# Weights of the last experts on the software queue, a GpSimd drain in another place, and an earlier token table

## Chip, cores, metric

One core of one Trainium2 chip. The metric is device microseconds (us) of one execution. Each execution is called fast, or slow when it took over 1.5% longer than the fastest of the same kernel in the same series.

## The reference

Causal attention over 4 batches of 8 heads (768 positions, head size 64); three heads attend to the whole past, five to 4 first positions and a window of 64. The result is the token matrix of a mixture of experts: each token goes to the one expert its domain id names.

```python
x = attn_out.transpose(0, 2, 1, 3).reshape(B * S, H * D)     # 3072 x 512
for e in range(8):
    mask = domain_id == e
    h = np.maximum(x[mask] @ w1[e], 0.0)                     # 512 -> 1024
    out[mask] = h @ w2[e]                                    # 1024 -> 512
```

## The kernel before

Attention runs over 16 pairs of heads (TensorE scores, ScalarE exponentials, TensorE again). VectorE works out a token table beside it (ranks of tokens in their experts). Then GpSimd gathers each expert's rows with indirect DMAs, TensorE does two layers, VectorE copies each group of 128 output rows from PSUM (the memory space in which the program places TensorE's results) into one of six buffers, which is called evacuation below (0.69 us each in the profile of before), and GpSimd scatters the group to its places with an indirect DMA. `nc.gpsimd.drain()` is an instruction whose record lasted 22.46 us in the profile of before, and GpSimd stood idle from 168.6 to 190.5 us. "Layer 1" and "layer 2" below are the two matrix products of an expert. Weights are 32-bit in memory and 16-bit where TensorE reads them. Either they are converted on the way by GpSimd's software queue (14 DMAs of 1024 KB each on the page of before), or, for w2 of experts 6 and 7, they come as they are through SyncE's hardware queue into spare buffers ("staged", eight DMAs of 512 KB) and VectorE casts them (eight casts of 0.69 us).

```python
opool = ctx.enter_context(tc.tile_pool(name="moe_out", bufs=6))
ps_b = ctx.enter_context(tc.tile_pool(name="ps_b", bufs=2, space=PSUM))
# ... (cut)
def w2_stage(e):
    for x in range(4):
        # ... (a spare tile of the attention half, as 32-bit)
        nc.sync.dma_start(out=stage_t[e, x], in_=src[:, x // 2, x % 2 * F : (x % 2 + 1) * F])

def w2_cast(e):
    # ...
    for x in range(4):
        nc.vector.tensor_copy(out=flat[:, x * F : (x + 1) * F], in_=stage_t[e, x])

def finish_group(pr, g, ps, o=None):
    o = opool.tile([P, DM], FP32, tag="oute", name=f"oute_{pr}_{g}")
    nc.vector.tensor_copy(out=o[:], in_=ps[:])               # the evacuation of PSUM
    inst = nc.gpsimd.indirect_dma_start(out=out, ..., in_=o[:])   # the scatter
# ...
after = {                                                    # (expert, group of layer 2) just done
    (0, 2): lambda: load_w(3, 2),
    (1, 2): lambda: ([load_xe(3, g) for g in range(4)], load_w(6, 1),
                     [load_xe(3, g) for g in range(4, NG)], load_w(7, 1)),
    (2, 0): lambda: w2_stage(6),
    (2, 2): lambda: (load_w(4, 2), load_w(5, 2)),
    (3, 2): lambda: (nc.gpsimd.drain(), w2_cast(6), w2_stage(7)),
    (5, 1): lambda: w2_cast(7),
}
```

`load_w(e, 2)` issues w2 of expert e on the software queue. A key such as (3, 2) is written below for a drain's place too: after expert 3's third group (groups are counted from 0); "h" is the group of leftover rows that two experts share. The layers of experts 0 to 3 alternate with layer 1 of 4 to 7; after layer 1 of expert 7 only layer 2 of experts 4 to 7 is left, and that is the stretch this study is about.

The softmax here doesn't subtract the row's maximum and nothing guards it: scores larger than these inputs give would overflow.

Of the kernel before, what the change touches and what calls it, by code (L numbers as in the profile page):

```python
# [9 lines left out]
FP16 = mybir.dt.float16  # L10
FP32 = mybir.dt.float32
# [6 lines left out]
P = 128  # L18
# [3 lines left out]
def kernel(  # L22
# [13 lines left out]
    nc = tc.nc  # L36
    B, H, S, D = q.shape
    NTOK, DM = out.shape
    E, _, F = moe_w1.shape
# [66 lines left out]
    c32_d = nc.inline_tensor(c32_np, "c32").ap()  # L106
# [3 lines left out]
    wpool = ctx.enter_context(tc.tile_pool(name="weights", bufs=4))  # L110
    qkpool = ctx.enter_context(tc.tile_pool(name="qk", bufs=3))
    vpool = ctx.enter_context(tc.tile_pool(name="v32", bufs=4))
    vepool = ctx.enter_context(tc.tile_pool(name="ve", bufs=2))
    tpool = ctx.enter_context(tc.tile_pool(name="qkT", bufs=2))
    epool = ctx.enter_context(tc.tile_pool(name="eT", bufs=5))
    xpool = ctx.enter_context(tc.tile_pool(name="xb", bufs=2))
# [3 lines left out]
    ps_s = ctx.enter_context(tc.tile_pool(name="ps_s", bufs=3, space=PSUM))  # L120
    ps_b = ctx.enter_context(tc.tile_pool(name="ps_b", bufs=2, space=PSUM))

    c16 = cpool.tile([P, c16_np.shape[1]], FP16, name="c16s")
    c32 = cpool.tile([P, c32_np.shape[1]], FP32, name="c32s")
    dom64 = cpool.tile([P, NT], I64, name="dom64")
# [9 lines left out]
    q32_t, qk_t, v_t, ve_t, w_t = {}, {}, {}, {}, {}  # L135
# [4 lines left out]
    def load_qk(n):  # L140
        b, pi = divmod(n, 4)
        hA, hB = PAIRS[pi]
        for nm, src in (("q", q), ("k", k)):
            t = qkpool.tile([P, 2, NSO, D], FP32, tag=nm, name=f"{nm}32_{n}")
            nc.sync.dma_start(
                out=t[:].rearrange("p h t d -> p h (t d)"),
                in_=hsel(src, b, hA, hB).rearrange("h (p t) d -> p h (t d)", p=P),
            )
            q32_t[nm, n] = t
# [10 lines left out]
    def load_v(b, pi):  # L160
        hA, hB = PAIRS[pi]
        t = vpool.tile([P, 2, NSO, D], FP32, tag="v32", name=f"v32_{b}_{pi}")
        for hh, h in enumerate((hA, hB)):
            nc.sync.dma_start(
                out=t[:, hh], in_=v[b, h].rearrange("(c p) d -> p c d", p=P)
            )
        v_t[b, pi] = t
# [15 lines left out]
    def load_vs(r, bh):  # L183
# [3 lines left out]
                0:NS, 2 * H * (bh + 1) - VH : 2 * H * (bh + 1), :  # L187
            ],
        )

    stage_t = {}

    def w2_stage(e):
        for x in range(4):
            pool, tag = ((xpool, "xb"), (vepool, "ve"))[x % 2]
            t = pool.tile([P, 2 * F], FP16, tag=tag, name=f"w2s_{e}_{x}")
            stage_t[e, x] = t[:].bitcast(FP32)
            nc.vector.memset(stage_t[e, x][0:1, 0:1], 0.0)
            src = moe_w2[e].rearrange("(c p r) d -> p c (r d)", p=P, r=4)
            nc.sync.dma_start(out=stage_t[e, x], in_=src[:, x // 2, x % 2 * F : (x % 2 + 1) * F])  # L200

    def w2_cast(e):
        t = wpool.tile([P, 2, 4, DM], FP16, tag="w1", name=f"w2_{e}")
        flat = t[:].rearrange("p c r d -> p (c r d)")
        for x in range(4):
            nc.vector.tensor_copy(out=flat[:, x * F : (x + 1) * F], in_=stage_t[e, x])  # L206
        w_t[e, 2] = t

    def load_w(e, which):
        if which == 1:  # L210
            t = wpool.tile([P, 2, 2, F], FP16, tag="w1", name=f"w1_{e}")
            nc.gpsimd.dma_start(
                out=t[:].rearrange("p c r f -> p c (r f)"),
                in_=moe_w1[e].rearrange("(c p r) f -> p c (r f)", p=P, r=2),
            )
        else:
            tag = "w2" if e < 6 else "w1"
            t = wpool.tile([P, 2, 4, DM], FP16, tag=tag, name=f"w2_{e}")
            nc.gpsimd.dma_start(
                out=t[:].rearrange("p c r d -> p c (r d)"),  # L220
                in_=moe_w2[e].rearrange("(c p r) d -> p c (r d)", p=P, r=4),
            )
        w_t[e, which] = t
# [75 lines left out]
    qT, kT, eT, avp, xb = {}, {}, {}, {}, {}  # L299
# [133 lines left out]
    def routing_items():  # L433
        V = nc.vector
        R = {}
# [192 lines left out]
        def rows3():  # L628
# [19 lines left out]

        lows = [lambda t=t: low(t) for t in range(0, NT, 4)]
        return {  # L650
            (0, 1): (one_hot,), (0, 2): (ranks, scan), (1, 0): (own,), (1, 1): (place,),
            (2, 0): (place2,), (3, 0): (split,), (4, 0): (flags, high), (4, 1): (high2, high3),
            (4, 2): lows[0:1], (5, 1): lows[1:2], (8, 0): lows[2:3], (8, 1): lows[3:4],
            (8, 2): lows[4:5], (9, 1): lows[5:6], (10, 0): (rows,), (11, 0): (rows2,),
            (12, 0): (rows3,),
        }

    xe_t, xT_t, hT_t = {}, {}, {}
# [139 lines left out]
    nc.scalar.dma_start(out=c16[:, 0:C_S0], in_=c16_d[:, 0:C_S0])  # L798
    load_qk(0)
    load_v(0, 0)  # L800
    load_qk(1)
    nc.sync.dma_start(out=c16[:, C_S0:], in_=c16_d[:, C_S0:])
    nc.sync.dma_start(out=dom64[:], in_=moe_domain_id.rearrange("(p c) -> p c", p=P))
    nc.sync.dma_start(out=c32[:], in_=c32_d)
    load_v(0, 1)
    load_qk(2)
    load_v(0, 2)
# [39 lines left out]
                load_xe(1, g, 3)  # L847

    def keep_warm(m, tag):
        ps = ps_s.tile([P, 1024], FP32, tag="sp", name=f"warm_{tag}")  # L850
        for _ in range(m):
            nc.tensor.matmul(
                out=ps[:, 0:DM], lhsT=zrow[:, 0:P], rhs=zrow[:], start=True, stop=True
            )
# [8 lines left out]
    for n in range(NPAIR + 1):  # L863
        if n < NPAIR:
            hooks(n)
        R = len(plans[n % 4]) // 2 if n < NPAIR else 1
        av0, av1 = av_items(n - 1) if n >= 1 else ([], [])
        tr = []
        if n == NPAIR:
            av0 = [lambda: keep_warm(4, "exp")] + av0  # L870
            av1 = av1 + [lambda: keep_warm(6, "last"), lambda: x_transpose(0, 0, 1, wide=True)]
        elif n + 1 < NPAIR:
            q_evac = nc.scalar.copy if R == 1 else nc.vector.tensor_copy
            tr = [lambda: transposes(n + 1, q_evac, R == 1)]
        if R == 1:
            run(tr)
        steps = {1: [av0 + av1], 2: [tr, av0 + av1], 3: [tr, av0, av1] if n else [[], [], tr]}[R]
        for x, step in enumerate(steps):
            if n < NPAIR:
                scores(n, (2 * x, 2 * x + 1))  # L880
            run(step)
            for fn in route.get((n, x), ()):
                fn()
# [25 lines left out]
    for g in range(4, NG):  # L909
# [16 lines left out]
            [load_xe(3, g) for g in range(4, NG)],  # L926
            load_w(7, 1),
        ),
        (2, 0): lambda: w2_stage(6),
        (2, 2): lambda: (load_w(4, 2), load_w(5, 2)),  # L930
        (3, 2): lambda: (nc.gpsimd.drain(), w2_cast(6), w2_stage(7)),
        (5, 1): lambda: w2_cast(7),
    }
    then = lambda *k: after.get(k, lambda: None)()
    for pr in range(E // 2):
# [20 lines left out]
    with tc.If(nc.values_load(flag_i[0:1, 0:1], min_val=0, max_val=2) > 0, preferred_fallthrough_block=False):  # L956
        x_v = x_d[1 : 1 + NTOK, :].rearrange("(b p s) d -> b s p d", b=B, p=P)
        with tc.For_i(0, B, 1) as gb, tc.For_i(0, NSO, 1) as gs:
            t = gb * NSO + gs
            g_d64 = rpool.tile([P, 1], I64, name="g_d64")  # L960
            nc.sync.dma_start(
                out=g_d64[:], in_=moe_domain_id[bass.ds(t * P, P)].rearrange("(p c) -> p c", c=1)
# [6 lines left out]
            for c in range(4):  # L969
                c1, r = divmod(c, 2)  # L970
                nc.tensor.transpose(
                    out=gps[:, c, :],
                    in_=gx[:, c1 * 256 + r : (c1 + 1) * 256 : 2],
# [5 lines left out]
            for e in range(E):  # L979
# [14 lines left out]
                ps = ps_b.tile([P, 512], FP32, tag="b", name=f"go2_{e}")  # L994
                for f in range(8):
                    nc.tensor.matmul(
                        out=ps[:],
# [7 lines left out]
                    out=hit[:], in0=g_dom[:], scalar1=float(e), scalar2=None, op0=ALU.is_equal  # L1005
# [46 lines left out]
```

## Time and profile before

| | kernel before |
|---|---|
| timed | 223.49 us, median of 3 executions (222.88 to 225.37) |
| its first profile, one execution | 214.84 us, span 213.0 us |
| first matmul of layer 1 | 91.9 us |
| last activation of layer 1 (hT of expert 7) | 176.0 us |
| GpSimd drain | 167.19 to 189.65 us |
| TensorE's last matmul ends | 206.1 us |
| last scatter issued | 207.61 us |

### The profile page before, as it was taken

The numbers are of one execution on the slowest core, as the hardware profiler recorded it, in microseconds if no ns is written. First come the engines' busy times: TensorE is split into PE (matmuls) and PEld (weight loads), VectorE is DVE, ScalarE is ACT, GpSimd is POOL, SyncE is SP. The second block draws the span as 40 slices with busy tenths as digits, with TensorE's granted clock in tenths as the row PEclk, the third lists the DMA queues.
The fourth block names the chain that finished last, engine by engine and source line by source line (L and its number), as shares of the span: only waits on it lengthen the run. The fifth ranks groups of instructions, "written<-read, shape, count | busy, mean of one in ns | idle before, by whom it ended". The sixth has DMA issues, their size and how long they took to land.

```text
span 213.0 us, 5417 instructions
## 1 busy us (share of the span) xinstructions
PE 186.8 (88%) x2250; PEld 123.5 (58%) x2250; DVE 100.7 (47%) x216; ACT 90.4 (42%) x115; POOL 117.4 (55%) x152
## 2 busy tenths in 40 slices
PE   7589986699999899985999999999999999894950
PEld 2247664387678567685898965455555664342430
DVE  4357989956897886520012225310353412263320
ACT  2466577247986986333465620056200561000000
POOL 7726759683346468771788445557763400027771
PEclk9757999669999999999799999999999999999996
DMA  6999999999999997999999999997999999804532
GB/s 185 299 277 276 300 246 271 285 331 268 281 305 294 346 325 143 222 173 297 242 200 196 262 245 215 279 257 194 210 190 325 332 228 309 339 12 149 194 142 98
DMA packets 45056, 51.86 MB, mean 244 GB/s; under 512 B 28895, under 2 KB 37472, under 8 KB 45026
## 3 DMA queue, kind: packets, MB, share of 16 engines
q0 software_dynamic: 8928, 24.70, 50.2%
q1 hardware_dynamic: 35954, 26.70, 43.2%
q8 instruction: 19, 0.31, 0.6%
q10 hardware_dynamic: 144, 0.07, 0.3%
q14 instruction: 11, 0.09, 0.2%
HBM read 56.73 MB, written 10.49 MB: 316 GB/s over the span
## 4 chain that ended last, share of the span: by engine, by line
DMA 38%; PE 23%; issue 17%; DVE 11%; POOL 4%; ACT 3%; POOLq 1%; SPq 0%; DVEq 0%; ACTq 0%
DMA w<-in_moe_w_dram 25%; PE av L402 6%; DMA k<-in_k_dram 5%; PE sp L348 5%; DMA out_dram<-oute,out_i 5%; PE o L772 3%; DMA xe<-x_tok,map_e 3%; PE sp L331 3%; ACT eT L359 3%; PE tp L312 2%; DVE xb L415 2%; POOL out_dram L738 2%; DVE kT L321 2%; DVE qT L321 1%; POOL xe L672 1%
## 5 line engine op out<-in xcount | busy, mean ns | idle before, releaser
L359 ACT ACTIVATE eT<-sp 128x1024 f16<-128x1024 f32 (+2 forms) x56 | 50.1, 953 | 17.5 <-PE sp L348 17.2
L729 ACT ACTIVATE hT<-h 128x512 f16<-128x512 f32 (+2 forms) x48 | 32.1, 668 | 57.9 <-PE h L722 57.9
L722 PE MATMUL h<-xT,w 128*128 128x256 f16 (+2 forms) x384 | 52.1, 297 | 1.3 <-DVE xT L707 0.8
L738 POOL DMA_INDIRECT out_dram<-oute,out_i x27 | 27.5, 1017 | 42.9 <-DVE w L206 21.9
L722 PEld LDWEIGHTS <-w 128*128 128x128 f16 x384 | 39.6, 115 | 12.4 <-issue 0.9
L772 PE MATMUL o<-w,hT 128*128 128x512 f16 x184 | 42.0, 379 | 3.2 <-DVE oute L736 3.2
L736 DVE COPY oute<-o 128x512 f32<-128x512 f32 x23 | 15.9, 691 | 46.9 <-PE o L772 32.9
L772 PEld LDWEIGHTS <-hT 128*128 128x128 f16 x184 | 17.5, 98 | 23.1 <-issue 4.3
L402 PEld LDWEIGHTS <-eT 128*128 128x128 f16 (+2 forms) x672 | 21.4, 102 | 7.4 <-issue 4.9
L402 PE MATMUL av<-ve,eT 128*128 128x65 f16 (+2 forms) x572 | 22.9, 198 | 2.4 <-DVE qT L321 0.7
L155 POOL CAST q<-q 128x768 f16<-128x768 f32 x15 | 13.5, 901 | 19.4 <-DMA q<-in_q_dram 9.1
L348 PE MATMUL sp<-qT,kT 64*64 64x128 f16 (+8 forms) x468 | 22.1, 259 | 0.8 <-DVE kT L321 0.8
L672 POOL DMA_INDIRECT xe<-x_tok,map_i x16 | 16.3, 1016 | 10.2 <-DMA x_tok<-xb 5.6
L707 DVE COPY xT<-xtp 128x1024 f16<-128x1024 f16 (+1 forms) x16 | 8.8, 552 | 24.6 <-PE xtp L694 24.6
L415 DVE TENSOR_TENSOR xb<-av,rcp 128x384 f16<-128x384 f32 x32 | 17.8, 557 | 1.1
L155 POOL CAST k<-k 128x768 f16<-128x768 f32 x15 | 12.6, 839 | 9.9 <-PE sp L348 5.7
L331 PE MATMUL sp<-c16s 128*128 128x128 f16 (+2 forms) x112 | 17.2, 271 | 0.8 <-ACT eT L359 0.7
L175 POOL CAST ve<-v 128x384 f16<-128x384 f32 x32 | 16.4, 540 | 0.0
L348 PEld LDWEIGHTS <-kT 64*64 64x64 f16 (+2 forms) x468 | 10.3, 105 | 8.9 <-issue 4.1
L764 ACT COPY oute_last<-o_last 128x128 f32<-128x128 f32 x2 | 0.5, 265 | 29.3 <-DVE oute_last L764 29.3
L331 PEld LDWEIGHTS <-c16s 128*128 128x128 f16 x112 | 8.4, 102 | 5.3 <-issue 3.0
L414 DVE RECIPROCAL rcp<-av 128x6 f32<-128x6 f32 x32 | 6.1, 191 | 9.9 <-PE av L402 8.7
(97 smaller groups left out, 179.5 us busy)
## 6 DMA issues: line engine op xcount, KB each, us to landing
w<-in_moe_w_dram POOLq DMA_DIRECT2D x14, 1024.0 KB, 12.1
q<-in_q_dram SPq DMA_DIRECT2D x16, 384.0 KB, 6.4
k<-in_k_dram SPq DMA_DIRECT2D x16, 384.0 KB, 6.3
v<-in_v_dram SPq DMA_DIRECT2D x32, 192.0 KB, 5.9
w2s<-in_moe_w_dram SPq DMA_DIRECT2D x8, 512.0 KB, 12.0
x_tok<-xb SPq DMA_DIRECT2D x4, 768.0 KB, 6.3
out_dram<-oute,out_i POOLq DMA_INDIRECT x27, 8.2
xe<-x_tok,map_i POOLq DMA_INDIRECT x16, 7.9
```

Of the source, the lines that this page charges most:

```text
L155: eng.tensor_copy(out=t[:].rearrange("p t h d -> p h t d"), in_=q32_t[nm, n][:])
L175: nc.gpsimd.tensor_copy(out=ve_t[b][:, :, h, 0:D], in_=v_t[b, pi][:, hh])
L331: nc.tensor.matmul(out=sp[:, c : c + w], lhsT=id_sb, rhs=c16[:, col : col + w], start=c // 512 not in begun, stop=True, skip_group_check=True,
L348: nc.tensor.matmul(out=sp[o : o + m, c : c + w], lhsT=kT[n][rows, k0 : k0 + m], rhs=qT[n][rows, i0 : i0 + w], start=False, stop=True, skip ...
L359: nc.scalar.activation(out=eT[n, r // 3][:, r % 3, c0:c1], in_=sp[:, c0:c1], func=AF.Exp, scale=scale)
L402: nc.tensor.matmul(out=ps[m0 : m0 + m, it, :], lhsT=eT[n, r // 3][rows, r % 3, c : c + m], rhs=rhs, start=(cell["n"] == 1), stop=(cell["n" ...
L415: nc.vector.tensor_tensor(out=xb[b][:, :, h * D : (h + 1) * D], in0=ps[:, :, 0:D], in1=rcp[:].unsqueeze(2).to_broadcast([P, NSO, D]), op=A ...
L672: nc.gpsimd.indirect_dma_start(out=xe_of(pr, g), out_offset=None, in_=x_d[0 : 1 + nb * S, :], in_offset=bass.IndirectOffsetOnAxis(ap=(map_ ...
L722: nc.tensor.matmul(out=pv[:, a, c0:c1], lhsT=w_t[e, 1][:, c // 2, c % 2, fc * 512 + fr : (fc + 1) * 512 : 4], rhs=xT_t[e][:, c, c0:c1], st ...
L729: nc.scalar.activation(out=hT_t[e][:, 2 * f2 : 2 * f2 + 2, c0:c1], in_=pv[:, :, c0:c1], func=AF.Relu)
L738: inst = nc.gpsimd.indirect_dma_start(out=out, out_offset=bass.IndirectOffsetOnAxis(ap=out_i[:, s : s + 1], axis=0), in_=o[:], in_offset=None,
L772: nc.tensor.matmul(out=ps[:], lhsT=hT_t[e][:, f, g * P : (g + 1) * P], rhs=w_t[e, 2][:, f // 4, f % 4, :], start=(f == 0), stop=(f == 7),)
```

## The change

Three intents: the part of the token table that clogs VectorE in pairs 3 to 5 goes half into the first pair, so its two loads go ahead of the second pair's, with warm-up matmuls for TensorE meanwhile; w2 of experts 6 and 7 comes through the software queue as all other weights do, so VectorE's casts go; and the drain comes between the scatters of expert 5.

```diff
-    def w2_stage(e): ...
-    def w2_cast(e): ...
@@ token table on VectorE, by (pair, step)
-            (0, 1): (one_hot,), (0, 2): (ranks, scan), (1, 0): (own,), (1, 1): (place,),
-            (2, 0): (place2,), (3, 0): (split,), (4, 0): (flags, high), (4, 1): (high2, high3),
+            (0, 0): (one_hot,), (0, 1): (ranks, scan, own, place, place2, split),
+            (1, 0): (high,), (2, 0): (high2,), (3, 0): (high3,), (4, 1): lows[0:1],
 ... (later entries cut)
@@ order of the loads
+    nc.sync.dma_start(out=dom64[:], in_=moe_domain_id.rearrange("(p c) -> p c", p=P))
+    nc.sync.dma_start(out=c32[:], in_=c32_d)
     load_qk(1)
     nc.sync.dma_start(out=c16[:, C_S0:], in_=c16_d[:, C_S0:])
-    nc.sync.dma_start(out=dom64[:], in_=moe_domain_id.rearrange("(p c) -> p c", p=P))
-    nc.sync.dma_start(out=c32[:], in_=c32_d)
@@ pair 0
-        steps = {1: [av0 + av1], 2: [tr, av0 + av1], 3: [tr, av0, av1] if n else [[], [], tr]}[R]
+        if n == 0:
+            tr, av0, av1 = [lambda: keep_warm(3, 0)], [lambda: keep_warm(3, 1)], tr
+        steps = {1: [av0 + av1], 2: [tr, av0 + av1], 3: [tr, av0, av1]}[R]
@@ after
-        (2, 0): lambda: w2_stage(6),
         (2, 2): lambda: (load_w(4, 2), load_w(5, 2)),
-        (3, 2): lambda: (nc.gpsimd.drain(), w2_cast(6), w2_stage(7)),
-        (5, 1): lambda: w2_cast(7),
+        (2, "h"): lambda: load_w(6, 2),
+        (3, 2): lambda: load_w(7, 2),
+        (5, 1): lambda: nc.gpsimd.drain(),
```

More of the change, by code (lines that the diff above doesn't have):

```diff
@@ L189, in load_vs @@
         )
-    stage_t = {}
-    def w2_stage(e):
-        for x in range(4):
-            pool, tag = ((xpool, "xb"), (vepool, "ve"))[x % 2]
-            t = pool.tile([P, 2 * F], FP16, tag=tag, name=f"w2s_{e}_{x}")
-            stage_t[e, x] = t[:].bitcast(FP32)
-            nc.vector.memset(stage_t[e, x][0:1, 0:1], 0.0)
-            src = moe_w2[e].rearrange("(c p r) d -> p c (r d)", p=P, r=4)
-            nc.sync.dma_start(out=stage_t[e, x], in_=src[:, x // 2, x % 2 * F : (x % 2 + 1) * F])
-    def w2_cast(e):
-        t = wpool.tile([P, 2, 4, DM], FP16, tag="w1", name=f"w2_{e}")
-        flat = t[:].rearrange("p c r d -> p (c r d)")
-        for x in range(4):
-            nc.vector.tensor_copy(out=flat[:, x * F : (x + 1) * F], in_=stage_t[e, x])
-        w_t[e, 2] = t
     def load_w(e, which):
@@ L650, in routing_items @@
         return {
-            (0, 1): (one_hot,), (0, 2): (ranks, scan), (1, 0): (own,), (1, 1): (place,),
-            (2, 0): (place2,), (3, 0): (split,), (4, 0): (flags, high), (4, 1): (high2, high3),
-            (4, 2): lows[0:1], (5, 1): lows[1:2], (8, 0): lows[2:3], (8, 1): lows[3:4],
-            (8, 2): lows[4:5], (9, 1): lows[5:6], (10, 0): (rows,), (11, 0): (rows2,),
-            (12, 0): (rows3,),
+            (0, 0): (one_hot,), (0, 1): (ranks, scan, own, place, place2, split),
+            (1, 0): (high,), (2, 0): (high2,), (3, 0): (high3,), (4, 1): lows[0:1],
+            (4, 2): lows[1:2], (5, 1): (flags,), (6, 0): lows[2:3], (7, 0): lows[3:4],
+            (8, 1): lows[4:5], (8, 2): lows[5:6], (10, 0): (rows,), (11, 0): (rows2,),
+            (12, 1): (rows3,),
         }
@@ L849, in keep_warm @@
     def keep_warm(m, tag):
-        ps = ps_s.tile([P, 1024], FP32, tag="sp", name=f"warm_{tag}")
+        pool, tag_, cols = (ps_b, "b", 512) if tag in (0, 1) else (ps_s, "sp", 1024)
+        ps = pool.tile([P, cols], FP32, tag=tag_, name=f"warm_{tag}")
         for _ in range(m):
```

## The prediction

> **What bounds the kernel now.** The kernel has two halves: attention for 16 head pairs, to about 90 us, then the eight experts. I read the busy slices first, then the chain that ended last, the waits, and the timelines of three stretches.
>
> ```profile
> PE   7589986699999899985999999999999999894950
> PEclk9757999669999999999799999999999999999996
> DMA  6999999999999997999999999997999999804532
> ```
>
> A slice is 5.3 us. TensorE is full from slice 18 on (96 us) until three dents at the very end: slices 35 (186 to 192 us), 37 and 39. The DMA engines are full from 5 us to about 181 us. So two things can set time: the DMA engines in the attention half, TensorE in the expert half, and whatever makes the dents. The busy table by stretch says the same: 81.5 of 85 us busy between 91 and 176 us, but 0.84 of 4 us between 191 and 195.
>
> In the chain (start, length, what) the dent has a cause:
>
> ```profile
> 167.19 1.41 POOLq L931
> 168.60 21.08 issue
> 189.69 0.03 POOLq L738
> ...
> 190.53 3.07 DMA out_dram<-oute,out_i
> ...
> 193.72 0.70 DVE oute L736
> ...
> 194.46 3.61 PE o L772 x16
> ```
>
> L931 is the drain on GpSimd. Its raw record lasts 22.46 us, from 167.19 to 189.65; the chain calls most of that "issue", and the wait list calls it a wait for a VectorE cast, but the program puts no wait on that cast there. The landing records say what was open meanwhile: the weights of experts 4 and 5 and four scatters, the last scatter landing at 187.07, and a staged part of w2 of expert 7 at 188.46. I take the drain to wait for the software queue to empty. Scatters of expert 4 that could go from 178.5 us on wait until 190.53; their six output buffers are then all in use, VectorE can't evacuate, and TensorE stops:
>
> ```profile
> PE o L772 <- DVE oute L736: 3.2, 1, 3.2
> PE o2h L786 <- DMA w<-in_moe_w_dram: 0.9, 1, 0.9
> DVE oute L736 <- DMA out_dram<-oute,out_i: 12.9, 6, 3.6
> ```
>
> (waiter, what ended the wait, us, times, longest). The first two are TensorE's losses there. Afterwards the backlog of 14 scatters goes out at GpSimd's own pace to the end:
>
> ```profile
> 203.75 0.98 POOL L738 DMA_INDIRECT out_dram<-oute,out_i  x1 [0.30 <-issue]
> 205.03 0.98 POOL L738 DMA_INDIRECT out_dram<-oute,out_i  x1 [0.30 <-DVE oute_last L764]
> 206.32 0.98 POOL L738 DMA_INDIRECT out_dram<-oute,out_i  x1 [0.30 <-issue]
> 207.61 0.98 POOL L738 DMA_INDIRECT out_dram<-oute_last,out_i  x1 [0.31 <-ACTq L956]
> ```
>
> One every 1.29 us, no gap. From the last issue at 207.61 to the end is 5.4 us of landing and exit.
>
> In attention, the routing table on VectorE between 30.1 and 38.4 us (8.3 us with two evacuations of q and k, 1.9 us, inside) stops TensorE, whose clock falls to 0.6 in slices 7 and 8. But look at what attention waits for later:
>
> ```profile
> 61.31 0.83 POOL L155 CAST k<-k 128x768 f16<-128x768 f32 x1 [0.99 <-DMA k<-in_k_dram]
> 62.10 0.50 PE L312 MATMUL tp<-c16s,q 128*128 128x128 f16 x6
> 62.44 0.50 PE L312 MATMUL tp<-c16s,k 128*128 128x128 f16 x6
> ```
>
> K of pair 11 lands at 61.16, is cast until 62.14, transposed at 62.44. By 62 us TensorE has caught up with the loads. The cast of q starts within 0.2 us of its landing in 13 of the 15 pairs that GpSimd casts.
>
> [...] software 50.2% and hardware 43.2% of the 16 engines' span, together 93%. [...] the scatters beside the staging casts took 1.18 and 1.31 us against 0.98. [...]
>
> **The change, part by part.**
>
> (a) Token table. Same VectorE work: one_hot to split goes before the evacuation of pair 1, high to high3 are spread over pairs 1 to 3, the 1.74 us flag to pair 5. Its loads (24 and 218 KB) go ahead of q and k of pair 1: before, they took the line from 11.98 to 12.76, so now c32 should land near 8.3 + 0.8 = 9.1 us. Then VectorE has about 24 small operations, some 7 us by their rows, and pair 1's qT comes near 17 instead of 13.86. That costs up to 3 us at pairs 1 and 2 and saves about 5 at 34 to 39 us. Neither should live: TensorE may be 5 us ahead by pair 9, and waits at 62.1 us for K of pair 11, whose landing the change doesn't move, because the bytes queued are the same. After that the slack to the loads is 0.1 us at pair 11, 0.4 at pair 12 and 0.5 at pair 15 (cast ended 79.68, transposes of q began at 80.17). The expert half then starts on the first gathered rows, which sit behind w1 of expert 1 (issued 80.53, after the last casts; landed 89.26). Sum: 0 to 0.5 us, say 0.2.
>
> (b) Warm-up matmuls. Six of 0.21 to 0.43 us in the first pair, where ScalarE sets the pace (six exponentials of 1.02 us). Under 0.5 us there, and again absorbed by the loads.
>
> (c) w2 of experts 6 and 7 on the software queue. Removes eight casts of 0.69 us and eight memsets from VectorE, all off the path. DMA time stays: weights on a filled software queue land every 4.8 to 5.4 us (w1 of expert 3 4.8; w1 of 4 and 5 in 10.7), scatters every 0.65 (139.19, 139.82, 140.43). From 158.5 us the old kernel had five weights and seven scatters to move: 5 x 5.1 + 7 x 0.65 = 30.1, so 188.6; it read 188.46, so the sum is sound. In the new order of the queue: w1 of 7 at 163.6, three scatters 165.5, w2 of 4 at 170.6, of 5 at 175.7, scatter, w2 of 6 at 181.5, three scatters 183.4, w2 of 7 at 188.5. Needed by TensorE at about 176, 181, 188 and 194. All in time, and the 0.9 us wait for w2 of 5 goes.
>
> (d) The drain after the scatter of expert 5's second group. The 3.16 us stop at 191.3 goes. Instead, six scatters of experts 4 and 5 queue behind w2 of 7: the first lands at 189.2 to 190.5, so the third evacuation of expert 5, ready at 188.5, is 1 to 2 us late, and TensorE, with two PSUM buffers, loses about 1 us. The drain then waits for the sixth: 188.5 + 6 x 0.65 = 192.4, plus 1 us as the 16 engines drift apart and 0.6 to 2.6 us as the two drains of the old trace ended after their last landing: 194 to 196. Eight scatters remain: first 0.9 us later, last 7 x 1.29 = 9.0 later, so 203.9 to 205.9. TensorE would end at 206.06 - 0.9 - 3.2 + 1 = 203.0 and its last scatter could go at 204.0, so GpSimd's chain still ends last. Against 207.61 the gain is 1.7 to 3.7, middle 2.9.
>
> Sum: 0.2 + 2.9 = 3.1 of the profile's 213.0 us, 1.5%. The timed runs are slower than the profiled one (223.49 against 214.84) for a reason the page doesn't tell; I carry the gain as a share: 223.49 x 0.985 = 220.1, said as 220.0.
>
> **The rivals.** First: attention gets faster by the 5 us VectorE clog. For it: TensorE's clock and busy slices there. Against it: the casts that start on their landings. It would make 214 to 215. Second: the wait only moves. With eight loads in one first-in-first-out queue the scatters wait for w2 of 7, and the drain in its new place holds eight scatters as the old one held fourteen. For it: scatters behind weights took 17 to 23 us to land at 159 to 167 us. If drain or weight come 4 us later than I have them, the gain is nil: 223 to 224. Third: the drain doesn't wait for landings but had another cause at 167 us, and costs little in its new place; then TensorE ends the kernel, last scatter at 204.0, gain 3.8: 219.5. Fourth: the late pair 1 is not absorbed and its 3 us stay: 222 to 223.
>
> **Range and chances.** Half of the weight lies on 1 to 2%. The first rival lifts the chance of over 2% to 0.34; only two failures together make it over 2% slower, 0.05. Range 215.5 to 223.5.
>
> **What would show it.** Right: the stop of TensorE for oute gone or near 1 us; a drain that begins near 188 and ends at 194 to 196; the last scatter issued at 204 to 206; the casts of k of pairs 11 to 15 at the same times within 1 us; the expert half starting within 0.5 us of 91.9. Wrong: first expert matmul before 90 us (the first rival), a TensorE wait on w of over 1 us after 176, a drain that ends after 198, or one of under 2 us.

## The result, and the profile after

In the first series the changed kernel took **216.98 us** (median of 4 executions, 216.26 to 218.19, all fast) against 223.44 us (median of 4, 222.88 to 225.37). The ratio is 0.970, 95% interval 0.963 to 0.978: faster by 3.0%. A ratio here is the mean time of one kernel's fast runs over that of the other's of the same rounds, so not quite the ratio of the medians.

The profile of the changed kernel from that series took 218.19 us, *longer* than the profile of before (214.84). So the two profiles can't be set side by side as they are. Its busy slices (tenths, 40 slices of 5.4 us) tell why:

```profile
PE   7671997899899897698999799999999999999940
PEclk9887579999999999559999999999999999999995
DMA  5999999999999988999349999999899999971242
```

Compare with the same rows of before in the prediction. (Slices are counted from 0 here. The prediction mixed two counts: the dents it shows are in slices 34, 36 and 38, and 36 is 192 to 197 us.) Those dents are gone: TensorE is at 9 from slice 23 to 37. But there is a new hole in slices 15 and 16, a half clock in 16 and 17, and the DMA engines lie half idle in 19 and 20. The timeline of TensorE in that execution (start, length, what, how often; in brackets the idle time before it and its releaser) shows a thin stream of work:

```profile
84.79 0.31 PE L384 MATMUL av<-ve,eT 128*128 128x65 f16 x5 [0.41 <-issue]
85.53 0.23 PE L384 MATMUL av<-ve,eT 128*128 128x65 f16 x2 [0.43 <-issue]
...
87.03 0.40 PE L384 MATMUL av<-ve,eT 64*128 64x65 f16 x6 [0.32 <-issue]
87.80 0.39 PE L384 MATMUL av<-ve,eT 64*64 64x65 f16 x6 [0.36 <-issue]
```

Bursts of five or six small matmuls every 0.75 us, and no wait that the profile names. Then the clock falls to half. The same by stretch (stretch, its length, busy us and counts of TensorE, weight loads, VectorE, ScalarE and GpSimd, then clock, DMA share, GB/s):

```profile
82.00:87.00 5.00, 3.44 (x79) 2.33 (x77) 1.61 (x3) 1.82 (x2) 3.69 (x5) 1.00 0.91 136
87.00:92.00 5.00, 3.37 (x47) 1.70 (x47) 1.50 (x4) 1.02 (x1) 4.08 (x6) 0.56 0.97 216
92.00:97.00 5.00, 4.77 (x59) 2.67 (x56) 1.07 (x4) 1.94 (x2) 2.79 (x3) 0.50 1.05 226
```

The last exponentials came at 93.57 and layer 1 began at 101.45 us. A second profile of the same kernel, taken later (c_after below, 210.44 us), has none of that:

```profile
PE   7681997999899989979789999999999999999940
PEclk9787579999999999999999999999999999999995
DMA  6999999999999988999969999999899999992143
```

Layer 1 began at 92.75 us there, against 91.91 in the first profile of before. So the hole is of one execution, not of the kernel. Both profiles agree on what follows layer 1, and there the changed kernel can be read. The group of layer 2's matmuls (count, busy us, mean ns, idle time before them and its releaser), which in the profile of before had lost 3.2 us to `oute`, is without a stop:

```profile
L754 PE MATMUL o<-w,hT 128*128 128x512 f16 x184 | 41.9, 379 | 0.0
```

The scatters on GpSimd in c_after, where the prediction showed those of before:

```profile
185.58 0.98 POOL L720 DMA_INDIRECT out_dram<-oute,out_i  x1 [0.84 <-DVE oute L718]
187.31 0.98 POOL L720 DMA_INDIRECT out_dram<-oute,out_i  x1 [0.74 <-DVE oute L718]
195.00 0.98 POOL L720 DMA_INDIRECT out_dram<-oute,out_i  x1 [6.70 <-issue]
...
204.03 0.99 POOL L720 DMA_INDIRECT out_dram<-oute_last,out_i  x1 [0.30 <-issue]
```

The 6.70 us of "issue" are the drain; its raw record runs from 187.08 to 194.12. Eight scatters follow, 1.29 us apart, and the last goes at 204.03 instead of 207.61. The chain of c_after shows TensorE going through to its last matmul:

```profile
163.61 12.11 PE h L704 x64
175.72 5.18 PE o L754 x24
180.90 1.85 PE o2h L768 x16
182.75 10.47 PE o L754 x48
...
198.62 0.89 PE o_last L738 x8
```

### The profile page after: what moved, and what is told of

The parts are those of the page before. It is cut to its first block, busy times and chain, and to the rows that moved or that the text cites.

```text
span 216.4 us, 5394 instructions
## 1 busy us (share of the span) xinstructions
PE 189.3 (87%) x2256; PEld 124.7 (58%) x2256; DVE 96.0 (44%) x200; ACT 89.6 (41%) x115; POOL 117.7 (54%) x154
## 4 chain that ended last, share of the span: by engine, by line
PE 77%; DVE 12%; issue 3%; ACT 2%; DMA 2%; POOL 2%; SPq 0%; POOLq 0%; ACTq 0%
PE h L704 23%; PE o L754 18%; PE av L384 10%; PE sp L330 8%; PE sp L313 4%; PE o2h L768 3%; PE xtp L676 3%; PE tp L294 2%; DVE kT L303 2%; DVE xb L397 2%; DMA k<-in_k_dram 2%; ACT eT L341 2%; POOL out_dram L720 2%; DVE ohh L556 1%; DVE qT L303 1%
## 5 line engine op out<-in xcount | busy, mean ns | idle before, releaser
L711 ACT ACTIVATE hT<-h 128x512 f16<-128x512 f32 (+2 forms) x48 | 31.3, 668 | 58.1 <-PE h L704 54.9
L704 PE MATMUL h<-xT,w 128*128 128x256 f16 (+2 forms) x384 | 50.7, 290 | 2.6 <-ACT hT L711 1.3
L704 PEld LDWEIGHTS <-w 128*128 128x128 f16 x384 | 39.0, 114 | 12.9 <-issue 2.3
L754 PE MATMUL o<-w,hT 128*128 128x512 f16 x184 | 41.9, 379 | 0.0
L384 PEld LDWEIGHTS <-eT 128*128 128x128 f16 (+2 forms) x672 | 22.7, 105 | 10.2 <-issue 7.3
L155 POOL CAST q<-q 128x768 f16<-128x768 f32 x15 | 12.4, 829 | 27.5 <-DMA q<-in_q_dram 15.4
L384 PE MATMUL av<-ve,eT 128*128 128x65 f16 (+2 forms) x572 | 24.3, 201 | 3.4 <-issue 1.5
```

The lines of the kernel that those rows point to most:

```text
L155: eng.tensor_copy(out=t[:].rearrange("p t h d -> p h t d"), in_=q32_t[nm, n][:])
L384: nc.tensor.matmul(out=ps[m0 : m0 + m, it, :], lhsT=eT[n, r // 3][rows, r % 3, c : c + m], rhs=rhs, start=(cell["n"] == 1), stop=(cell["n" ...
L704: nc.tensor.matmul(out=pv[:, a, c0:c1], lhsT=w_t[e, 1][:, c // 2, c % 2, fc * 512 + fr : (fc + 1) * 512 : 4], rhs=xT_t[e][:, c, c0:c1], st ...
L711: nc.scalar.activation(out=hT_t[e][:, 2 * f2 : 2 * f2 + 2, c0:c1], in_=pv[:, :, c0:c1], func=AF.Relu)
L754: nc.tensor.matmul(out=ps[:], lhsT=hT_t[e][:, f, g * P : (g + 1) * P], rhs=w_t[e, 2][:, f // 4, f % 4, :], start=(f == 0), stop=(f == 7),)
```

## The experiments

Because attention varies by up to 9 us between executions, I compare the expert half by its own clock: from the last activation of layer 1 (the moment expert 7's `hT` is begun) to TensorE's last matmul, and to the end of the span. Every quoted profile enters that table with these two distances:

| profile (us) | w2 of 6 and 7 | drain | layer 1 begins | last hT | last hT to TensorE's end | last hT to the end |
|---|---|---|---|---|---|---|
| before, first profile | staged | (3,2) | 91.9 | 176.0 | 30.0 | 37.0 |
| c_before | staged | (3,2) | 90.8 | 174.5 | 31.7 | 38.4 |
| attn_only | staged | (3,2) | 93.0 | 175.4 | 31.3 | 38.4 |
| before_nodrain | staged | none | 92.1 | 175.9 | 28.3 | 37.4 |
| drain_moved (slow) | staged | (5,1) | 94.8 | 177.6 | 28.3 | 36.6 |
| stage_7_only | 7 staged | (5,1) | 91.9 | 176.7 | 27.7 | 35.5 |
| moe_old_drain | queue | (3,2) | 92.2 | 175.8 | 32.7 | 39.0 |
| drain_early | queue | (1,2) | 91.7 | 176.1 | 30.9 | 37.4 |
| moe_nodrain | queue | none | 91.3 | 175.1 | 25.5 | 34.7 |
| moe_only | queue | (5,1) | 91.3 | 175.6 | 25.5 | 32.7 |
| moe_only2 (slow) | queue | (5,1) | 95.8 | 179.7 | 25.5 | 33.7 |
| after, first profile | queue | (5,1) | 101.5 | 183.1 | 25.5 | 33.3 |
| c_after | queue | (5,1) | 92.8 | 175.8 | 25.5 | 32.8 |
| c_after2 | queue | (5,1) | 92.7 | 175.5 | 25.5 | 32.9 |

In the six profiles of the last rows, of three different kernels, TensorE needs 25.5 us: that is this stretch without a stop, and the slow execution among them is no exception. The timed results, in four series on two chips (all "before" executions of a series are shared):

| kernel | executions, us | fast runs over fast runs of before | 95% |
|---|---|---|---|
| c_before | 213.68 to 215.36 | 0.999 | 0.991 to 1.006 |
| attn_only | 215.57 to 218.30 | 1.011 | 1.002 to 1.020 |
| moe_only | 210.10 to 218.72 | 0.983 | 0.974 to 0.991 |
| moe_only2 | 209.82 to 215.22 | 0.983 | 0.973 to 0.992 |
| c_after | 210.44 to 218.71 | no ratio given | |
| c_after2 | 210.16 to 220.05 | 0.986 | 0.974 to 0.999 |
| drain_moved | 211.56 to 217.44 | 0.984 | 0.970 to 0.999 |
| moe_nodrain | 211.52 to 217.52 | 0.982 | 0.970 to 0.995 |
| moe_old_drain | 215.66 to 217.37 | 1.002 | 0.992 to 1.013 |
| before_nodrain | 212.66 to 215.82 | 0.991 | 0.979 to 1.003 |
| drain_early | 212.15 to 215.52 | 0.994 | 0.984 to 1.003 |
| stage_7_only | 213.02 to 214.45 | no ratio given | |

The kernel before itself ran between 210.90 and 222.53 us in these series. For the expert half, timing alone doesn't tell moe_only (0.983) from drain_moved (0.984) or moe_nodrain (0.982). What follows about its causes rests on the stretch table and the waits, one profile for each kernel and run.

### 1. Controls: both kernels again

No edit. 

> Control, the kernel before, unchanged, with a profile of its own. The first profile of it ran 214.84 us while its four timed runs took 222.88 to 225.37. Theory A (the one profile was a lucky execution: in a typical one TensorE loses some 9 us in the last attention pairs, as the profile of the changed kernel shows at 82 to 101 us): this profile runs 222 to 225 us, its first expert matmul comes near 100 instead of 91.9, and its drain, 22 us long before, is still over 14 us. Theory B (the timed runs pay about 9 us outside the profiled span, whatever the execution): this profile runs near 215 again with the first expert matmul near 91.9, and the timed runs near 223.4. Timed: 223.4 either way.

> Control, the changed kernel, unchanged. Timed near 217.0. Theory A: its profile varies between executions too; if it escapes the loss in the last attention pairs it runs near 208, first expert matmul near 92; if not, 216 to 218 with the first expert matmul near 101. Theory B: the loss of 9 us at 82 to 101 us is a property of the change (attention ends later), so it comes back at 101 and 217 in every profile of this kernel and in none of the kernel before.

Measured: c_before took 213.68 to 215.36 us, its profile 214.61, with layer 1 at 90.78. c_after took 210.44 (the profile) and then 218.71, 215.65 and 215.05, which makes three of its four executions slow ones.

Both my theories fall. Theory A said that a typical execution of before has the hole: it doesn't here. Theory B said that the profile and the timed runs of before differ by nature: on this chip they agree. What is left is that executions of either kernel differ by up to 9 us and more, and that those of the first series were all long (before by 8 to 10.5 us against its profile, after by 6 to 8 against c_after's 210.44). The profiles in which attention lost nothing visible read 212.8 and 213.0 before, 208.6 and (c_after2) 208.4 after: 4.4 us, **2.1%**. "Undisturbed" below means these profiles. It doesn't mean the fastest execution that is possible: one unprofiled execution of before took 210.90 us (in the series of stage_7_only), less than any of its profiles and only 0.7 more than the fastest of the changed kernel (210.16).

### 2. The two parts alone

attn_only keeps the token table, load order and warm-up lines of the diff above; moe_only keeps the weights and the drain. 

> Kernel before with the attention part of the change alone (order of the token table, its two loads ahead of pair 1, warm-up matmuls in pair 0); w2 of experts 6 and 7 staged and the drain as before. My prediction: attention is set by its loads, gain 0 to 0.5 us, so about 223.2. Rival 1 (attention gets faster by the 5 us VectorE clog): 218 to 219. Rival 4 (the late pair 1 isn't absorbed): 225 to 227.

> Kernel before with the expert part alone (w2 of experts 6 and 7 on the software queue, drain after expert 5's second group), attention as before. My prediction: gain of 2.9 us in the expert half, 220.5. If the changed kernel's expert half of 105.4 us against 114.2 of the first profile of before is the whole effect of this part: gain 6 to 8.7 us, 215 to 217.5. Rival 2 (the wait only moves): 223 to 224.

Measured: attn_only 1.011, moe_only 0.983. The profile of moe_only took 210.10 us with a span of 208.3, that of the whole change 210.44 and 208.6. So, in these profiles, the expert part is the whole gain. The attention part gains nothing. It trades one stop of TensorE for another: moe_only has one of 3.0 us before the transposes at 39 us, with the clock at half from 38.9 to 45.7; c_after has one of 5.4 us at 15 to 20 us, for kT of pair 1 from VectorE, with the clock at half from 18.4 to 28.6. Layer 1 begins 1.5 us *later* in c_after than in moe_only (92.75 and 91.25), but the last hT comes only 0.2 us later (175.75 and 175.56). Where the 1.5 us go, TensorE's waits between 91 and 113 us tell (us, times, longest). First moe_only, then attn_only:

```profile
PE xtp L676 <- DMA xe<-x_tok,map_e: 3.0, 3, 1.3
```

```profile
PE xtp L694 <- DMA xe<-x_tok,map_e: 2.0, 1, 2.0
```

An earlier TensorE waits longer for the gathered rows. In c_after that wait is 1.9 us. So the 1.5 us that are left at the end of attention are absorbed by the first gathers behind it. The timed runs say more: the fast runs of attn_only are 2.3 us slower than those of before, with an interval (1.002 to 1.020) that excludes no effect. I had expected a gain of 0 to 0.5 us, and a loss of 1.6 to 3.6 was my rival 4. So there was no gain, but "neutral" is shown for the profiles alone.

### 3. Drain moved, or taken out

drain_moved, against the kernel before:

```diff
-        (3, 2): lambda: (nc.gpsimd.drain(), w2_cast(6), w2_stage(7)),
-        (5, 1): lambda: w2_cast(7),
+        (3, 2): lambda: (w2_cast(6), w2_stage(7)),
+        (5, 1): lambda: (w2_cast(7), nc.gpsimd.drain()),
```

> Kernel before with one edit: the drain moved from expert 3's third group to expert 5's second; w2 of experts 6 and 7 still staged on the hardware queue and cast by VectorE. Theory (the drain's place is the whole gain of the expert part): TensorE's stop of 3.2 us for oute gone, drain starts at 186 to 188 and, with 4 MB less in front of it on the software queue, ends by 190 to 193, last scatter issued 203 to 204.5, profile 208 to 209 where nothing else disturbs the execution, against 212.8 to 213.0. Rival (the w2 loads on the software queue are needed for it): stop of TensorE stays over 2 us, or a wait for w2 of expert 5 to 7 appears, profile 211 to 213.

Measured: the 3.2 us stop for `oute` is gone, yet from the last hT to the end it took 36.6 us, hardly less than before. The profile fell in a slow execution, but its clock was at full speed from 65.8 to 209.2 us, so all through layer 2, and its stops have names:

```profile
178.11 5.35 PE L772 MATMUL o<-w,hT 128*128 128x512 f16 x24 [0.59 <-DMA w<-in_moe_w_dram]
...
184.84 1.89 PE L786 MATMUL o2h<-w,hT 128*64 128x512 f16 x15 [1.04 <-DMA w<-in_moe_w_dram]
...
194.23 3.61 PE L772 MATMUL o<-w,hT 128*128 128x512 f16 x16 [0.50 <-DVE oute L736]
```

TensorE waited for w2 of experts 4 and 5, and once for evacuations held up by the four casts (2.65 us on VectorE). That is the rival I had written: the weights on the software queue are needed for it. The timed fast runs (0.984, interval 0.970 to 0.999) are too wide to tell this kernel from moe_only, so the same has to show in a fast execution.

before_nodrain is the kernel before without `nc.gpsimd.drain()`. 

> Kernel before with the drain taken out and nothing else. Theory (the drain alone made the stop and the backlog): stop of TensorE for oute gone, last scatter issued 202 to 203, profile 206.5 to 208, some 5 to 6 us under the kernel before, more than the whole change gains. Rival (the scatters of expert 4 are late anyway, behind the weights on the software queue): a stop of 1 to 3 us stays, profile 209 to 212.

Measured, in a fast execution: last scatter at 205.23 us, span 213.4. A wait of 1.9 us for w2 of expert 5 is there, and the 0.50 us behind the casts:

```profile
183.25 1.89 PE L786 MATMUL o2h<-w,hT 128*64 128x512 f16 x15 [1.86 <-DMA w<-in_moe_w_dram]
...
192.65 3.61 PE L772 MATMUL o<-w,hT 128*128 128x512 f16 x16 [0.50 <-DVE oute L736]
```

TensorE's part, 28.3 us, is that of drain_moved. The theory "the drain alone" falls; the rival was right that stops stay, though it named late scatters and the larger stop was for the weight.

moe_nodrain is moe_only without its drain. 

> Kernel with the expert part of the change alone and the drain taken out altogether. Theory (the drain only costs; in its new place it lasts 7.0 us and leaves a backlog of 8 scatters that GpSimd sends out at its own pace until 203.8, 2.8 us after TensorE's last matmul at 201.0): last scatter issued at 202.0 to 202.8, 1 to 1.8 us sooner than with the drain, profile 206.5 to 207.5. Rival (the drain buys something at the end, as the last landings): last scatter sooner, but from it to the end over 5.5 us instead of 4.5, profile 208 or more.

Measured: the last scatter went at 201.46, even sooner than the theory said, and the profile took 211.52 us, span 209.8, 1.5 us *more* than with the drain. From the last issue to the end it was 8.3 us instead of 4.5. My rival was right: the drain buys something at the end. On GpSimd:

```profile
198.91 0.98 POOL L720 DMA_INDIRECT out_dram<-oute,out_i  x1 [0.74 <-DVE oute L718]
201.46 0.98 POOL L720 DMA_INDIRECT out_dram<-oute_last,out_i  x1 [1.57 <-DVEq L937]
```

What follows is the drain with which the program ends: 202.34 to 208.89 in the raw record, though the last data of the software queue had landed at 204.66. So I took all drains of the traces, and measured from the last landing of the software queue to the drain's end, against the number of DMAs that GpSimd had issued since the last drain:

```
DMAs since the last drain   us from the last landing to the end of the drain
  8 or 9                    0.71 0.80 0.82 0.82 0.83 0.85 0.91
 15 or 16                   1.07 1.08 1.08 1.09
 28                         1.57
 50                         2.95
 61 or 62                   2.92 2.92 2.93 2.98
 67 to 69                   3.28 3.59 3.61 3.88 4.23 4.31 4.38
 76 or 78                   4.12 4.24
```

The drains of this list ended 0.71 to 4.38 us after the last landing: some 0.4 us plus about 0.05 us for each DMA since the last drain (my estimate from this list; it gives 3.5 us for 61, where 2.9 were measured). The row of 67 to 69 doesn't fit it: these seven drains, all at (5, 1), lasted 7.01 to 7.12 us from begin to end, whether the last landing came 2.6 us after their begin (the first profile of after) or 3.8 (c_after). There the landing didn't set the end, and what did stays open. Nor do the traces tell the number of DMAs from what grows with it, such as the pieces that they consist of. That still gives a reason to have a drain before the end: 69 of 78 DMAs lie before the drain at (5, 1), beside which TensorE still works, and the last drain has eight left (0.71 to 0.91 us after the last landing in the list, against 4.12 and 4.24 after 76 or 78). The gain of 1.5 us is read from two profiles on different chips; the timed ratios (0.982 without the drain, 0.983 with it) show none.

### 4. The drain left in its old place

moe_old_drain is moe_only with `(3, 2): lambda: (load_w(7, 2), nc.gpsimd.drain())` and none at (5, 1). 

> Expert part of the change, but the drain left at expert 3's third group, right behind the issue of w2 of expert 7. Theory (the drain waits for all that is open on the software queue, w2 of expert 7 last): it starts near 167 and ends within 3 us of the landing of w2 of expert 7, 186 to 191; TensorE stops for oute for 3 us or more, profile 212 to 215, no gain or a loss against before. Rival (it was a cause tied to the staged casts on VectorE, which are gone here): drain under 10 us, no stop, profile 208 to 209.

Measured: the drain ran from 166.37 to 189.97, 23.6 us, 3.0 us beyond the last landing at 186.99. Ratio 1.002: the whole gain is gone. The timeline of TensorE, and for comparison that of c_before:

```profile
194.50 6.07 PE L754 MATMUL o<-w,hT 128*128 128x512 f16 x16 [4.67 <-DVE oute L718]
```

```profile
191.65 4.85 PE L772 MATMUL o<-w,hT 128*128 128x512 f16 x11 [3.16 <-DVE oute L736]
```

The theory was right; the rival, a cause tied to the casts, falls. And the stop costs more than its length in two of three profiles. In the first profile of before, 16 such matmuls took 3.61 us after a stop of 3.16 us, at a granted clock of 1.00 (from 103.8 to 209.7 us). Here 16 took 6.07, and in c_before 11 took 4.85 (the view ends at 196 us; all 16 took 6.50): the clock had fallen. It reads 5 in slice 36 of both (193 to 199 us here, 192 to 197 in c_before); all 184 matmuls of layer 2 took 44.9 us in c_before and 41.9 in c_after.

So stops of the same length, 3.16 us, were followed by half the clock in c_before and by a full one in before. The clock records of before begin and end on a grid of 3.41 us. Of the 2.48 us stop before the transposes at 39.31 us, 2.2 us lie in the one step of that grid that ends at 39.0, and the clock was at half from 39.0 to 45.8 us. The stop of 3.16 us (191.3 to 194.5 us) lies across two steps, 1.3 and 1.9 us. In drain_early the clock reads 7 in slice 35 (187 to 192 us), after a stop of 2.59 us that ended at 188.52. What decides between the two outcomes isn't shown by these few stops.

### 5. Which staged load does it

stage_7_only has the drain at (5, 1) and w2 of expert 6 on the software queue; only w2 of expert 7 is staged and cast.

```diff
-        (2, 0): lambda: w2_stage(6),
+        (2, "h"): lambda: load_w(6, 2),
-        (3, 2): lambda: (nc.gpsimd.drain(), w2_cast(6), w2_stage(7)),
-        (5, 1): lambda: w2_cast(7),
+        (3, 2): lambda: w2_stage(7),
+        (5, 1): lambda: (w2_cast(7), nc.gpsimd.drain()),
```

> Kernel before with the drain moved to expert 5's second group and w2 of expert 6 on the software queue; only w2 of expert 7 is still staged and cast by VectorE. With both staged, the moved drain left 36.6 us from the last first-layer activation to the end (before 37.0 to 38.4; whole expert part 32.7 to 33.7), TensorE waited 0.6 and 1.0 us for w2 of experts 4 and 5, and w2 of expert 5 landed near 184.8 - 3.5 on the scale of an undisturbed execution, against 175.9. Theory (the staged load of w2 of expert 6, issued at 151 to 156 on the hardware queue, is what slows the weights that are needed sooner): with it gone, no wait for w2 of experts 4 and 5 over 0.2 us, 33.3 to 34.5 us from the last first-layer activation to the end, only a stop of up to 0.6 us left where the four casts of expert 7 hold up two evacuations. Rival (staging either of them costs alike, through the casts and the shared engines): 35.5 to 36.6 us, a wait for w stays.

Measured: half of each. No wait for a weight is left, and w2 of expert 5 landed at 178.6 us, where before_nodrain has it at 183.2 and drain_moved at 184.8. That is the theory's part. But it took 35.5 us from the last hT to the end, the rival's figure, because the stops moved:

```profile
186.97 5.34 PE L772 MATMUL o<-w,hT 128*128 128x512 f16 x24 [1.48 <-DVE oute L736]
192.81 3.61 PE L772 MATMUL o<-w,hT 128*128 128x512 f16 x16 [0.50 <-DVE oute L736]
```

The staged w2 of expert 7 landed from 173.9 to 184.6 beside the software queue's work, so w2 of expert 6 landed at 185.4 instead of 180.7 (moe_only), and the three scatters queued behind it at 186 to 187.4. Their buffers weren't free for the evacuations. The six executions took 213.02 to 214.45, all fast; the four fast ones of moe_only2 209.82 to 212.51.

The landings show what the second queue took from the first, whose data were due sooner: w2 of expert 5 landed at 183.2 us beside the staged load of expert 6 (before_nodrain), at 178.6 without it. In the one queue the weights landed in the order in which they were issued (163.5, 170.3, 175.1, 181.2 and 188.0 us in c_after), which here is the order in which they are needed. The order is what differs, not the amount: all of w1 of expert 7 and w2 of 4 to 7 had landed at 188.1 us in before_nodrain and at 187.4 in moe_only. One reservation: with expert 6 out of the way, expert 7's staging began 9 us earlier than in before (165.3 against 174.3 us), so this run doesn't price each of the two loads as it stood in before.

### 6. An earlier drain, as a try for a faster kernel

If a drain costs its landing time plus a time for each DMA, it might be cheaper where GpSimd has slack. drain_early is moe_only with the drain between the last gathers and w1 of expert 7.

```diff
             [load_xe(3, g) for g in range(4, NG)],
+            nc.gpsimd.drain(),
             load_w(7, 1),
-        (5, 1): lambda: nc.gpsimd.drain(),
```

> Expert part of the change with the drain put earlier: in expert 1's third group, after the last gathers and before the issue of w1 of expert 7. Theory (a drain ends when the software queue's open transfers have landed, plus a time that grows with the number of DMAs GpSimd issued since the last drain: 0.8 us after 8, 1.1 after 15, 2.9 after 61, 3.3 to 4.4 after 67 to 69, 4.2 after 76 to 78 in the ten traces so far, so about 0.4 + 0.05 us for each): it starts near 151.5, the last gathers land near 158, some 50 DMAs are cleared, so it ends near 161 and lasts 9 to 10 us; w1 of expert 7 lands 4 to 5 us later than 164 and TensorE still doesn't wait for it; last scatter issued at 202.0 to 202.6, as without a drain (201.46); some 27 DMAs are cleared at the end, so the last landing is followed by about 1.7 us of drain instead of 4.2; profile 206.0 to 207.3, under the expert part with its drain (208.3) and without one (209.8). Rival (no slack before w1 of expert 7, or the held-up scatters fill their six buffers): TensorE stops by 1 to 4 us between 158 and 175, profile 208 to 211.

Measured: the sum for the drains held (2.95 us after the last landing with 50 DMAs, 1.57 at the end with 28), but the rival came: ratio 0.994, span 213.5. The drain began at 147.9 us and lasted 11.7, longer than my 9 to 10. GpSimd was idle for 9.08 us, from 151.12 to 160.20, and the software queue moved no data from 156.7 to 161.7 us. The following loads landed about 6 us later than in moe_only (w2 of expert 4 at 176.5 instead of 170.8, of expert 6 at 187.0 instead of 180.7), the scatters with them, and TensorE stopped:

```profile
176.57 5.35 PE L754 MATMUL o<-w,hT 128*128 128x512 f16 x24 [0.53 <-DMA w<-in_moe_w_dram]
...
188.52 10.48 PE L754 MATMUL o<-w,hT 128*128 128x512 f16 x40 [2.59 <-DVE oute L718]
```

So there is no slack in the software queue of 5 us at 157 us. Of the three places tried, only the one behind the issue and the landing of nearly all weights, (5, 1), left TensorE without a stop.

### 7. The expert part and the whole change once more

> The expert part alone once more, with more rounds, beside the whole change in the same call: is the attention part worth anything? Profiles that nothing disturbed read 208.3 (expert part alone) and 208.6 (whole change). Theory (attention part neutral, its 1.5 us of later attention absorbed in the first layer of the first experts): fast runs 210 to 212, within 1 us of the whole change. Rival (the attention part costs in most executions): expert part alone 2 us or more faster than the whole change.

> The whole change once more with more rounds: 210 to 212 in undisturbed executions and 215 to 219 in the others, before 213.5 to 215 and 216 to 219. If the 3.0% of the first measurement was the change's own, the ratio is 0.97 again; if it was 2.0% (4.4 of 213 us, the difference of the undisturbed profiles) plus the luck of which executions were disturbed, it is 0.975 to 0.99.

Measured: fast runs of moe_only2 209.82, 210.89, 211.29 and 212.51, mean 211.1; of c_after2 210.16, 211.84, 211.98 and 213.16, mean 211.8. They agree within 1 us, as the theory of a neutral attention part says. But that compares the fast runs, which were picked by their time. Over both series 7 of the 12 executions of the whole change were slow and 3 of the 10 of the expert part alone; the medians of all are 215.4 and 211.9. So the rival, that the attention part costs 2 us or more in most executions, isn't excluded: whether the change brings slow executions about or merely met more of them, no profile of one in these series tells. c_after2's ratio was 0.986, as expected of a change whose own gain is near 2%. No version beat the change clearly; moe_only, the expert part alone, is at least as fast with less code.

The profile of moe_only2 was a slow execution, and most of its loss sits in attention: layer 1 begins 4.5 us later than in moe_only, of 5.2 in all (columns by stretch as above):

```profile
53.00:58.00 5.00, 3.53 (x77) 2.21 (x72) 3.90 (x8) 4.22 (x6) 0.54 (x1) 1.00 1.10 284
58.00:64.00 6.00, 5.65 (x65) 4.49 (x66) 2.23 (x5) 1.62 (x2) 4.16 (x8) 0.54 1.12 284
```

TensorE was 30% idle before 58 us and then ran at half clock. drain_moved has the same at 59 to 64 us, the first profile of after at 87 to 97 us. What starts it in one execution and not in the next I couldn't settle.

## Why the prediction was right or wrong

The time came within the range: 216.98 us for 215.5 to 223.5. The largest chance, 0.61, was on "within 2%", and the first series said 3.0% faster, twice the 1.5% that I had worked out. That the time still lies in the range is in part luck: the profiles give the change 2.1%, and the rest of the 3.0% has no explanation. Step by step:

**(a) Token table, 0.2 us.** About zero in the profiles (208.6 us with it, 208.3 without), but not for the reason given, and a loss of 2.3 us in the timed runs of attn_only. I had pair 1 late by up to 3 us, and K of pair 11, set by the loads, to absorb it. The qT of pair 1 came at 18.46 us in c_after, not near 17 (before: 13.86). The loads did come as I said: the casts of k of pairs 11 to 15 began within 0.7 us of those of c_before (against the first profile of before they were 1.3 to 1.9 us early). But TensorE didn't wait for them: after 59 us the wait lists of before and of c_after name no cast of k, so the wait at 62.1 us that I read from the timeline wasn't one. The lateness shrank because the stop at 36 to 39 us went, not because of the loads; the expert half still began 0.8 us late in c_after against the first profile, 1.5 against moe_only, and the gathers took that up. The first rival, attention faster by 5 us, which had lifted the chance of "faster" to 0.34, didn't come: that chance was given for a wrong reason.

**(b) Warm-up matmuls.** They weren't tried alone. The 0.21 to 0.43 us that I gave for each are the distances of the warm-up matmuls in the profile of before: 0.216 us at 87 us, 0.427 at 2 to 4 us. They didn't keep the clock up: it was at half from 18.4 to 28.6 us in c_after, having fallen during the 5.4 us stop at pair 1.

**(c) Weights on the software queue: "all off the path".** This is the step of the expert half that failed. The landing times were right: w2 of 4 to 7 at 170.6, 175.7, 181.5 and 188.5 predicted, 170.3, 175.1, 181.2 and 188.0 in c_after. Wrong was to count only the 0.9 us wait for w2 of expert 5 as tied to it. With the drain out of the way and both loads staged, TensorE still lost 2.4 us (before_nodrain: 1.9 and 0.5) and took 28.3 us for a stretch of 25.5. I had reckoned that DMA time stays. So it did (the last weights landed at 187.4 us through one queue, at 188.1 through two), but the move makes an order, and the order was what counted (w2 of expert 5 landed at 183.2 us beside the staged load of expert 6, at 178.6 without it). Cast work on VectorE, called off the path, cost 0.5 us there. The longer scatters beside casts that the prediction noted come back in each profile with casts looked at (before, c_before, before_nodrain, drain_moved, stage_7_only): a scatter begun beside them took 1.18 to 1.31 us, others there 0.98 to 1.07.

**(d) The drain, 2.9 us.** Its times were right: begin near 188, end 194 to 196, last scatter 203.9 to 205.9 predicted; 187.1, 194.1 and 204.0 measured. But two errors cancelled there. The last landing came at 190.8 in c_after, not at 192.4 to 193.4, and the drain ended 3.3 us after it, not 0.6 to 2.6. (The 1 us for engines that drift apart was an estimate; in the profile of before, the first and the last of a scatter's 16 landing marks lay 4.6 to 4.9 us apart in the four scatters that landed between 178 and 188 us.) The mechanism was incomplete: a drain doesn't only wait for landings; what follows the last landing is longer after more DMAs (0.71 to 0.91 us after 8 or 9, 4.12 and 4.24 after 76 or 78; the list above, with its exception). A slip besides: the middle of 1.7 to 3.7 is 2.7, not 2.9. Two more terms were mis-sized. The loss of "about 1 us" of TensorE to late scatters was 0.0: VectorE waited 1.7 us for a buffer and two PSUM buffers hid it. And "5.4 us of landing and exit" was 4.6: 0.3 us less in the last drain after its landing (eight DMAs since the one before instead of 15), 0.2 from an earlier landing, 0.3 after the drain.

**The sum.** 3.6 us from the scatters and 0.8 us from the exit make 4.4 of 213.0 us, 2.1%, where I had 3.1 and 1.5%. The remaining part of the first series' 3.0% isn't the change's as far as the profiles show: its executions of both kernels were 6 to 10 us longer than undisturbed ones, and the later repeat (c_after2) gave 1.4%. That part is open, as no profile of a 223 us execution of before exists.

**The rivals.** The second (the wait only moves) happened in the experiments, not in the change: moe_old_drain and drain_early are such moves. The third (the drain doesn't wait for landings) fell with moe_old_drain, 23.6 us long without any staged cast. The fourth (3 us of pair 1 stay) didn't come in the profiles, where 1.5 us stayed to the end of attention and 0.2 to the last hT; attn_only's timed 2.3 us are within what it said, so it isn't refuted.

## What to carry to other kernels

Moving loads to a second queue added no bandwidth here (the last weights landed at 188.1 us with two queues, at 187.4 with one), but it took some from what was due sooner (w2 of expert 5 landed at 183.2 us, at 178.6 without the staged load of expert 6); where transfers are needed in a known order, one queue in that order can be worth more than two (here 25.5 us against 28.3 from the last hT to TensorE's end, both without a drain). Two fixes may each give little and together 4 us (from the last hT to the end: 36.6 us with the drain moved alone, 39.0 with the queue alone, 32.7 with both, 37.0 to 38.4 with neither), so undo both singly before naming the cause. And when executions vary more than the effect, measure a stretch by its own start and end in the trace, rather than the whole.
